# Batch 5's q by TensorE, batch 1's convolution on VectorE, four one-batch tap buffers and a new order in a fused attention and gated-convolution kernel

## The chip, the core and the metric

The kernel runs on one core of a Trainium2 chip. A core has TensorE (PE in the profile; it multiplies matrices into PSUM, and its loading of the stationary operand is listed as PEld), VectorE (DVE), ScalarE (ACT), GpSimd (POOL), SyncE (SP, here a queue for DMAs alone) and 16 DMA engines that move data between HBM and SBUF. Each engine works through its own queue of instructions in order, and engines wait for one another by semaphores. The metric is the device time of one execution in microseconds, the median of several runs.

## What is computed

The inputs are q, k, v of shape (8 batches, 8 heads, 576 tokens, 64), a norm weight g, and three weights of a gated convolution layer, all float32; the output is (8, 576, 512) float32.

```python
kv  = einsum('bhsd,bhse->bhde', k, v)              # linear attention, no softmax
out = einsum('bhsd,bhde->bhse', q, kv)
rms = sqrt(mean(out * out, axis=-1) + 1e-6)        # over the 64 of a head
x   = (out / rms * g) -> (batch, 576, 512)         # heads side by side
h   = maximum(x @ w_in, 0)                         # 512 -> 1024
conv = sum_k conv_w[k] * h shifted by k - 1 tokens # 3 taps, each channel by itself
y   = (h * sigmoid(conv)) @ w_out                  # 1024 -> 512
```

## The kernel before

All products are bf16 with float32 sums. The eight batches go through the same steps, and four pairs of batches share one x and one h buffer. Two heads fill the 128 rows of a tile, so a batch has four tiles t of x; h has eight tiles f of 128 channels.

The program is a list of small functions (`@op`, lines 216 to 795) and one string, `ORDER` (line 67). A token such as `kv.3.0.4@2` calls `kv(3, 0, 4)` with buffer or PSUM bank number 2; `:1` chooses the other engine for a step that ScalarE and VectorE can both do. Each engine issues its part of the tokens exactly in this order (lines 807 to 815 chain the instructions of an engine), so the string decides all that lies behind what. The number of a slot decides which earlier use of a buffer must have ended first.

The tokens, in the order of a batch's way:

- `Lq`, `Lk`, `Lv`, `Li`, `Lo`: loads of q, k, v (two buffers each) and of w_in and w_out, issued on POOL's queue, which also converts to bf16. Batch 0 is loaded in pieces by `pre`, batch 1 in halves.
- `unread`: products of a constant tile whose result nobody reads; `unread.3` is three of them (line 427).
- `kv` (line 358): sums of k times v over tokens; `kvc`, `kvn`, `ky` copy them from PSUM, `kx` moves halves by DMA.
- q must be turned so that its 64 is on the partitions. `qt0` and `qt` do it on TensorE (line 380), one token of six at a time; `qtp` does it two tokens at a time (line 388) for batches in `QP`; `dq` does it by a DMA transpose on SP's queue (line 436) for batches in `QD`. `qc0` and `qc` copy the turned q from PSUM.
- `ot` and, for batches in `QUAD` (both ways that give pairs of tokens), `oq` (line 464): q times kv. `sq` squares on ScalarE, `oc` copies the product to a float32 buffer (ring `o32`).
- The norm: batches 0 and 1 by `on`, `nl`, `mu0`. The others by `ss` (sums of squares, line 575), `ln` (reciprocal root on ScalarE), `sl` (VectorE splits the factors), `sp` (TensorE spreads them over partitions, line 603) and `mu` (VectorE multiplies, line 629). `dq`'s batch 7 gets its factors by DMAs (`fw`, `fr`).
- `hm` (line 640): eight products of w_in for one tile f; `re` is the relu (ScalarE, or VectorE with `:1`).
- The convolution works on a pair of tiles f: `ta` makes the two outer taps of one tile (VectorE), `aa` and `ab` add them and h, `sg` is the sigmoid (ScalarE), `mg` multiplies h by it (VectorE). `CONV` has five groups: batch 0, batch 1 and the pairs 2-3, 4-5, 6-7. Tiles 6 and 7 of batches 0 and 1 go another way: `cm` (line 731) makes the sum of taps on TensorE with diagonal matrices (`dg`), and `sg` reads it from PSUM.
- `om` (line 761): eight products of w_out for 128 rows of output, in two halves of four for the first and the last pair; `ea` copies the sum (ring `row`), `st` stores it on SP's queue. `oh`, `eh`, `sh` do the last rows in two column halves.

ScalarE loads a table when it goes from `nl` or `ln` to `sg` or back (line 213). The taps lie in two buffers for two batches each:

```python
taps = [consts.tile([P, 2, 2, 2, TW], BF16, name=f"taps{i}") for i in range(2)]
...
T["tap", c, f // 2] = taps[slots.pop(0)]
```

Of the kernel before, what the change touches and what calls it, by code (L numbers as in the profile page):

```python
# [59 lines left out]
QD = (5, 6, 7)  # L60
QP = (4,)
# [6 lines left out]
pre@0,0,0 unread.10@0 qt0.0.0@0 ps pn pi ca.k.0 ca.v.0 kv.0.0.1@1 kvc.0.0.1.0:1@0 ct@2 qt0.0.1@3 qc0.0.0:1@0  # L68
kvc.0.0.1.1 ot.0.0@0 qc0.0.1:1 unread.3@4 kv.0.1.1@3 Lq.1.0@1 pg sq.0.0@0 on.0.0@4 al.x0@0 al.h1@0 nl.0.0@0 pc
dg.7:1 kvc.0.1.1.0:1 dg.6:1 unread.1@6 qt0.0.2@2 kvc.0.1.1.1:1 ot.0.1@6 unread.3@3 kv.0.2.1@3 sq.0.1@1 mu0.0.0  # L70
al.x1@1 Li.1 al.h0@1 kvc.0.2.1.0:1 Li.3 qc0.0.2:1@1 kvc.0.2.1.1:1 on.0.1@4 nl.0.1@1 qt0.0.3@2 Lv.1.0@1 ot.0.2@0
mu0.0.1 sq.0.2@2 qc0.0.3:1 unread.3@3 kv.0.3.1@4,5 kvc.0.3.1.0 on.0.2@6 kvc.0.3.1.1:1 nl.0.2@2 ot.0.3@4 mu0.0.2
sqh.0.3.0@3 unread.3@3 onh.0.3.0@6 sqh.0.3.1 onh.0.3.1 nlh.0.3.0@3 muh.0.3.0 Lk.1.0@1 qt.1.0@0 nlh.0.3.1 qc.1.0:1@2
muh.0.3.1 Li.0 hm.0.2@6 re.0.2 ta.0.2@0 hm.0.3@4 re.0.3 hm.0.6@6 Lq.1.2 ta.0.3 Lv.1.2 re.0.6 aa.0.1 hm.0.7@4 Lk.1.2
Lq.2.0@0 cm.0.6@6 re.0.7:1 sg.0.6@1 kv.1.0.2@0 cm.0.7@4 kvc.1.0.2.0:1@1 kvc.1.0.2.1 sg.0.7 ot.1.0@0 hm.0.1@6 ab.0.1
sq.1.0@4 re.0.1 qt.1.1@4 hm.0.0@2 on.1.0@6 mg.0.3 qc.1.1@3 ot.1.1@4 nl.1.0@4 re.0.0:1 sq.1.1@5 kv.1.2.2@2
kvc.1.2.2.0 ta.0.0@1 mu0.1.0 kvc.1.2.2.1 on.1.1@6 Li.2 ot.1.2@2 nl.1.1@5 ot.1.3@0 ta.0.1 sq.1.2@6 mu0.1.1 aa.0.0
unread.1@6 on.1.2@6 sq.1.3@7 ab.0.0 nl.1.2@6 mu0.1.2 on.1.3@4 nl.1.3@7 Lk.2.0@0 qt.2.0@6 sg.0.3 qt.2.1@4 mu0.1.3
ha.1.2@2 hb.1.2 qc.2.1@4 sg.0.2 qc.2.0@0 ha.1.3@0 hb.1.3 re.1.2 re.1.3 hm.1.7@4 Lv.2.0@0 hm.0.4@2 mg.0.1 Lq.3.0@1
hm.0.5@0 sg.0.1 Lk.3.0@1 Lv.3.0@1 re.1.7 sg.0.0 pl ta.1.2@0 re.0.4 ta.1.3 re.0.5 hm.1.4@4 kv.2.0.4@2 Lo.0 aa.1.1  # L80
ab.1.1 mg.0.0 sg.1.3 sg.1.2 kvc.2.0.4.0@0 hm.1.5@0 kvc.2.0.4.1 ta.0.4@1 ta.0.5 ot.2.0@2 mg.1.1 aa.0.2 hm.1.6@6
re.1.4 ot.2.2@4 re.1.5 sq.2.0@0 ta.1.4@0 ab.0.2 re.1.6 qt.3.1@0 oc.2.0:1@0 qt.3.0@6 qc.3.1@1 hm.1.1@2 ot.2.1@0
# [10 lines left out]
st.0.0 ab.2.2 ta.2.6@0 sg.2.5 re.3.1 re.3.2 ta.2.7 oq.4.3@6 oq.4.2@0 sg.2.4 re.2.3 kv.5.0.4@5 sq.4.2@2 Lv.7.0@0
Lk.7.0@0 om.0.6.4 om.0.5.0@2 aa.2.3 ab.2.3 Lk.6.0@1 Lv.6.0@1 kvn.5.0.4 sq.4.3@3 oc.4.2@0 mg.2.2 ky.5.0.4.0:1
ea.0.6@4 ss.4@3 dq.7.0@1 oc.4.3 ky.5.0.4.1:1 oq.5.0@0 oq.5.1@4 sq.5.0@4 ta.2.2@1 om.0.5.4 sq.5.1@5 oc.5.0:1@2
om.0.4.0@6 oc.5.1 ta.2.3 oq.5.3@0 oq.5.2@4 aa.2.1 om.0.8.0@7 ea.0.5@5 ab.2.1 sq.5.3@6 om.0.4.4 sq.5.2@7 ss.5 ln.2@0
om.0.8.4 hm.2.1@2 oc.5.2@3 ea.0.8@6 oc.5.3 re.2.1 sl.2@0 hm.2.0@4 sp.4.1@0,2 ea.0.4@7 om.0.7.0@7 re.2.0 mu.4.1.0
mu.4.1.1 sp.4.0@4,0 kv.7.0.4@6 mu.4.0.0 sg.2.2 mu.4.0.1 om.0.7.4 kvn.7.0.4:1 sg.2.3 ea.0.7@2 sp.5.0@4,2 hm.3.0@0
al.h2@1 re.3.0 kx.7.0.4.0 dq.7.1@4 mu.5.0.1 mu.5.0.0 hm.4.5@2 re.4.5 sp.5.1@6,4 hm.4.1@0 mg.2.1 mu.5.1.0 hm.4.2@2
mu.5.1.1 ta.2.0@1 sg.2.7 hm.4.0@6 hm.5.3@4 ta.2.1 re.4.1 sg.2.6 mg.2.3 kx.7.0.4.1 re.4.0 re.4.2 oq.7.0@0 re.5.3  # L100
kv.6.0.4@6 oq.7.1@4 sq.7.0@0 hm.5.2@2 oc.7.0@1 aa.2.0 Lq.6.0@1 hm.4.3@0 st.0.4 dq.6.0@2 sq.7.1@1 oc.7.1 re.5.2
hm.4.4@4 st.0.5 kvn.6.0.4:1 ab.2.0 ta.3.2@0 re.4.3 hm.5.6@0 st.0.1 ta.3.3 hm.5.4@2 hm.5.1@6 sg.2.1 sg.2.0 re.4.4
re.5.6 re.5.1 re.5.4 hm.5.0@4 oq.7.3@6 oq.7.2@0 aa.3.1 re.5.0 mg.2.0 om.1.6.0@2 om.1.3.0@3 ab.3.1 st.0.3 kx.6.0.4.0
st.0.6 ta.3.0@1 dq.6.1@3 sq.7.3@2 sq.7.2@3 ta.3.1 sg.3.3 sg.3.2 hm.5.5@4 oc.7.2@0 st.0.7 aa.3.0 ss.7@0 mg.3.1 ln.4@0
al.x3@1 ab.3.0 ta.3.4@0 ea.1.3@7 re.5.5 om.1.1.0@1 oc.7.3 ea.1.6@5 kx.6.0.4.1 om.1.0.0@0 fw.4 fr.7.0@0 ea.1.1@0
oq.6.0@2 oq.6.2@6 oq.6.3@4 om.1.8.0@1 ta.3.5 ea.1.0@1 sq.6.2@4 fr.7.1@1 oc.6.2@2 oq.6.1@6 aa.3.2 om.1.4.0@0 sq.6.0@5
sq.6.3@6 sq.6.1@7 oc.6.0@3 ss.6@2 ab.3.2 oc.6.1 ea.1.8@4 ln.3@0 ea.1.4@2 hm.4.6@6 om.1.5.0@2 oc.6.3 sl.3@0 st.1.0
# [738 lines left out]
```

## Time and profile before

| | |
|---|---|
| three runs | 179.43, 179.44, 180.92 us |
| span of the profiled execution | 177.6 us |
| TensorE, busy | 168.4 us |
| ScalarE, busy | 149.7 us |
| VectorE, busy | 139.5 us |
| granted TensorE clock, every slice | 9 (90% or more of full speed) |

The span is the time from the first to the last instruction that the profiler recorded; the times of runs are those of whole executions, so they lie somewhat above it. Matmuls are pipelined and the profile models their ends, so mean times of single products overlap, and the step from one to the next is shorter. The chain of waits follows the work that ended last back to its start and gives start and length of each piece. In rows of groups stand line, engine, operation, output<-input, shapes, count, then busy time, mean ns of one, and idle time before them with what ended it.

### The profile page before, as it was taken

What the parts mean: (1) busy time and instruction counts of PE and PEld (TensorE: products, weight loads), DVE (VectorE), ACT (ScalarE), POOL (GpSimd) and SP (SyncE); (2) the same over time, 40 slices, a digit from 0 to 9 for tenths busy, and PEclk for the clock granted to TensorE, in tenths of its full rate; (3) what the DMA queues carried; (4) which work ended last, traced back from release to release, by engine and by line L of the source; (5) the groups of instructions that cost most, each with busy time, mean ns of one, the idle gap of its engine ahead of it and who ended that gap; (6) DMA issues with size and microseconds to landing.
All of it is one profiled execution on the core that took longest, in us unless ns stands there. A gap on an engine that the chain in (4) does not pass through costs nothing.

```text
span 177.6 us, 4060 instructions
## 1 busy us (share of the span) xinstructions
PE 168.4 (95%) x1641; PEld 101.3 (57%) x1660; DVE 139.5 (79%) x235; ACT 149.7 (84%) x233; POOL 30.8 (17%) x54
## 2 busy tenths in 40 slices
PE   6989996999999999999999999999999999999992
PEld 2545753877545677753667764444677764444541
DVE  5665669999998898999799999939999999950000
ACT  2479899999999969999999999999989987764332
POOL 7995516402600013050000000000000000000000
PEclk9999999999999999999999999999999999999999
DMA  6999999999999999999999950197040003422696
GB/s 155 188 183 197 200 204 201 205 203 206 205 204 203 198 192 139 174 203 198 160 201 179 293 128 0 53 219 263 21 160 0 4 0 143 152 82 99 258 352 219
DMA packets 36219, 29.49 MB, mean 166 GB/s; under 512 B 8528, under 2 KB 31720, under 8 KB 36200
## 3 DMA queue, kind: packets, MB, share of 16 engines
q0 software_dynamic: 21760, 15.96, 59.5%
q1 hardware_dynamic: 14400, 13.26, 28.9%
q8 instruction: 13, 0.21, 0.4%
q14 instruction: 6, 0.05, 0.1%
q10 hardware_dynamic: 40, 0.01, 0.0%
HBM read 33.70 MB, written 9.58 MB: 244 GB/s over the span
## 4 chain that ended last, share of the span: by engine, by line
PE 70%; DMA 20%; POOL 4%; ACT 2%; issue 2%; POOLq 0%; ACTq 0%
PE bank L761 33%; PE bank L640 27%; DMA v_sb<-in_v_dram 10%; DMA k_sb<-in_k_dram 7%; DMA q_sb<-in_q_dram 4%; PE bank L358 3%; PE bank L464 2%; POOL q_sb L241 1%; PE bank L603 1%; PE bank L575 1%; POOL v_sb L241 1%; POOL k_sb L241 1%; PE bank L776 1%; PE bank L731 1%; PE bank L388 1%
## 5 line engine op out<-in xcount | busy, mean ns | idle before, releaser
L640 PE MATMUL bank<-xT,w_in_sb 128*128 128x288 bf16 x496 | 64.5, 286 | 0.1
L761 PE MATMUL bank<-w_out_sb,h 128*128 128x512 bf16 x268 | 63.0, 379 | 1.1 <-issue 0.6
L640 PEld LDWEIGHTS <-w_in_sb 128*128 128x128 bf16 x496 | 47.6, 98 | 14.1 <-issue 0.5
L761 PEld LDWEIGHTS <-h 128*128 128x128 bf16 x280 | 26.3, 98 | 30.6 <-issue 1.9
L646 ACT ACTIVATE h<-bank 128x576 bf16<-128x576 f32 x61 | 37.9, 657 | 4.2 <-PE bank L640 3.9
L745 ACT ACTIVATE taps<-taps,cwn 128x1152 bf16<-128x1152 bf16 (+1 forms) x36 | 38.2, 1094 | 0.1
L341 ACT ACTIVATE row<-bank 128x512 f32<-128x512 f32 (+1 forms) x37 | 21.3, 598 | 12.3 <-PE bank L761 9.3
L751 DVE TENSOR_TENSOR h<-h,taps 128x2304 bf16<-128x2304 bf16 (+1 forms) x20 | 22.2, 1113 | 2.0 <-ACT taps L745 1.2
L706 DVE TENSOR_TENSOR taps<-taps 128x2304 bf16<-128x2304 bf16 (+1 forms) x18 | 20.9, 1160 | 0.4
L712 DVE TENSOR_TENSOR taps<-taps,h 128x2304 bf16<-128x2304 bf16 (+1 forms) x18 | 20.8, 1153 | 0.3
L699 DVE TENSOR_SCALAR taps<-h,cwn 128x1152 bf16<-128x1152 bf16 (+1 forms) x36 | 16.7, 463 | 2.5 <-ACT h L646 2.4
L493 ACT ACTIVATE sq<-bank 128x576 bf16<-128x576 f32 x28 | 17.9, 676 | 0.0
L700 DVE TENSOR_SCALAR taps<-h,cwn 128x1152 bf16<-128x1152 bf16 (+1 forms) x36 | 17.5, 487 | 0.0
L629 DVE SCALAR_TENSOR_TENSOR xT<-o,cw,bank 128x576 bf16<-128x576 f32 x20 | 15.3, 809 | 2.7 <-PE bank L603 2.5
L341 ACT ACTIVATE o<-bank 128x576 f32<-128x576 f32 x22 | 15.0, 694 | 0.0
L213 ACT ACT_TABLE_LOAD x10 | 12.8, 1283 | 2.5 <-issue 2.4
L301 POOL DMA_DIRECT2D q_sb<-in_q_dram x8 | 6.2, 772 | 31.4 <-PE bank L388 16.6
L427 PE MATMUL bank<-fill 128*128 128x512 bf16 x25 | 9.0, 480 | 1.7 <-DVE fill L228 1.5
L358 PEld LDWEIGHTS <-k_sb 96*64 96x64 bf16 x384 | 7.3, 114 | 4.0 <-issue 2.6
L358 PE MATMUL bank<-v_sb,k_sb 96*64 96x64 bf16 x384 | 8.5, 199 | 1.0 <-DMA k_sb<-in_k_dram 0.7
L301 POOL DMA_DIRECT2D k_sb<-in_k_dram x8 | 6.1, 758 | 14.4 <-PE bank L358 12.5
L562 DVE SCALAR_TENSOR_TENSOR xT<-bank,cw,root 128x576 bf16<-128x576 f32 x7 | 5.6, 815 | 1.8 <-ACT root L542 1.7
(93 smaller groups left out, 135.3 us busy)
## 6 DMA issues: line engine op xcount, KB each, us to landing
out_dram<-row SPq DMA_DIRECT2D x35, 256.0 KB, 2.8
q_sb<-in_q_dram POOLq DMA_DIRECT2D x6, 576.0 KB, 13.7
k_sb<-in_k_dram POOLq DMA_DIRECT2D x6, 576.0 KB, 14.7
v_sb<-in_v_dram POOLq DMA_DIRECT2D x6, 576.0 KB, 16.3
factor<-factor SPq DMA_DIRECT2D x4, 288.0 KB, 4.9
w_in_sb<-in_moe_w_in_dram POOLq DMA_DIRECT2D x4, 256.0 KB, 8.7
w_out_sb<-in_moe_w_out_dram POOLq DMA_DIRECT2D x2, 512.0 KB, 18.0
q_sb<-in_q_dram POOLq DMA_DIRECT2D x4, 144.0 KB, 4.6
```

The costliest lines, as they stand in the source:

```text
L341: nc.scalar.activation(to, fr, AX.Copy)
L358: nc.tensor.matmul(ps[i][i * D:(i + 1) * D, t - t0, :], k_sb[:, 2 * t + i, r * D:(r + 1) * D], v_sb[:, 2 * t + i, r * D:(r + 1) * D], star ...
L493: nc.scalar.activation(in_order(b, s), product(b, t), AX.Square)
L640: nc.tensor.matmul(ps[:, e, :HS], w_in_sb[:, t, f * P:(f + 1) * P], x[:, t, e * HS:(e + 1) * HS], start=(t == 0), stop=(t == NT - 1))
L646: nc.scalar.activation(to, fr, AX.Relu)
L699: nc.vector.tensor_scalar_mul(tap[:, 0, f % 2, :n, 8:8 + S], h[:, f], cwn[:, 0, f:f + 1])
L700: nc.vector.tensor_scalar_mul(tap[:, 1, f % 2, :n, :S], h[:, f], cwn[:, 2, f:f + 1])
L706: nc.vector.tensor_add(tap[:, 1, :, :n, :S], tap[:, 0, :, :n, 7:7 + S], tap[:, 1, :, :n, 1:1 + S])
L712: nc.vector.tensor_add(y, y, h[:, 2 * j:2 * j + 2])
L745: nc.scalar.activation(y, y, AX.Sigmoid, scale=cwn[:, 1, f:f + 1])
L751: nc.vector.tensor_mul(h, h, T["tap", c, j][:, 1, :, :n, :S])
L761: nc.tensor.matmul(T["om", p, m], h[:, f, m * P:(m + 1) * P], w_out_sb[:, f, :], start=(f == 0), stop=(f == NF - 1))
```

## The change

Batch 5 goes from `QD` to `QP`: its q is turned on TensorE two tokens at a time, and copied by two `qc`, instead of two DMA transposes. The sum of taps of batch 1's tiles 6 and 7 is made on VectorE by `ta`, `aa`, `ab` like the others, instead of `cm` on TensorE. The tap buffers become four for one batch each; a group of two batches takes two that are neighbours. Output rows 0 to 511 of the last pair go to the float32 buffers of `oc`. The whole order is written anew: among other things fifteen groups of unread products (39 in all) stand where eight groups (27) stood, and ScalarE's table changes twelve times, not ten.

```diff
-QD = (5, 6, 7)
-QP = (4,)
+QD = (6, 7)
+QP = (4, 5)
...
 ORDER = """
-pre@0,0,0 unread.10@0 qt0.0.0@0 ps pn pi ca.k.0 ca.v.0 kv.0.0.1@1 kvc.0.0.1.0:1@0 ct@2 qt0.0.1@3 qc0.0.0:1@0
...
-oc.2.1 Lk.4.0@0 Lv.4.0@0 kv.3.0.4@2 re.1.0 ss.2@3 oc.2.3 mg.0.2 ln.8@0 aa.1.2 kvc.3.0.4.0:1@1 kvc.3.0.4.1:1 ab.1.2
...
-om.0.2.0@2 Lv.5.0@1 sg.1.5 sg.1.4 qtp.4.0@0 cm.1.6@6 qc.4.0@4 mg.1.2 ea.0.0@2 hm.2.5@4 sl.1@0 hm.2.2@0 sg.1.1
-om.0.2.4 re.2.5 sg.1.6@0 re.2.2 ea.0.2@3 sg.1.0 sp.3.0@6,4 cm.1.7@0 mu.3.0.1 mu.3.0.0 hm.2.4@2 hm.2.7@6 sg.1.7
...
-st.3.2 st.3.0 st.3.7 eh.3.8.1 sh.3.8.1
+pre@0,0,0 unread.10.0@0 ca.v.0 Lq.1.0@1 unread.3.5@1 pi ca.k.0 qt0.0.0@0 unread.1.3@1 kv.0.0.1@2 qc0.0.0@0
...
+sq.2.1@3 qc.3.0@0 ss.2@4 kv.3.0.4@5 qc.3.1@1 ln.8@0 hm.1.1@6 kvc.3.0.4.0@0 ab.1.1 kvc.3.0.4.1 oc.2.0:1@1 Lo.1 sl.8@0
...
+om.0.2.0@6 om.0.2.4 qtp.4.0@2 sg.1.0 ta.1.5 mu.2.0.0 Lv.4.0@0 mu.2.0.1 ea.0.2@3 sl.1@0 qtp.5.1@0 ab.1.3 qtp.5.0@4
...
+kvn.4.0.4 hm.2.6@2 mu.3.1.1 ky.4.0.4.0:1 re.2.6 Lq.7.0@1 qtp.4.1@0 ky.4.0.4.1:1 hm.3.4@4 sg.1.6 qc.4.1@3 sg.1.5 re.3.4
...
+sg.4.5 ta.4.7 om.3.2.0@2 st.2.4 st.1.1 ea.2.8@3 om.2.2.0@6 sg.4.4 aa.4.3 st.2.5 om.3.7.0@3 ab.4.3 ea.2.0@2 om.3.5.0@4
+ea.2.2@4 sg.4.7 om.3.4.0@5 sg.4.6 om.3.3.0@6 mg.4.2 ea.2.1@6 om.3.1.0@7 st.1.0 st.2.2 om.3.0.0@1 ea.2.3:1@0 mg.4.3
+om.3.0.4 st.2.6 om.3.5.4 om.3.3.4 om.3.7.4 ea.3.5:1@4 ea.3.0@0 oh.3.8.0@0 om.3.1.4 st.2.7 ea.3.7:1@1 ea.3.3@1 om.3.4.4
...
+oh.3.8.1 ea.3.4:1@3 st.3.1 st.3.4 st.3.2 ea.3.6@4 eh.3.8.1:1 st.2.3 st.3.6 sh.3.8.1
 """
...
+    def units(n):
+        s = slots.pop(0)
+        return taps[:, s:s + n].rearrange("p b k f w -> p k f b w")
...
-    taps = [consts.tile([P, 2, 2, 2, TW], BF16, name=f"taps{i}") for i in range(2)]
+    taps = consts.tile([P, 4, 2, 2, TW], BF16, name="taps")
...
-        for t in taps:
-            nc.vector.memset(t[:, 0, :, :, 7:8], 0.0)
-            nc.vector.memset(t[:, 1, :, :, S:S + 1], 0.0)
+        nc.vector.memset(taps[:, :, 0, :, 7:8], 0.0)
+        nc.vector.memset(taps[:, :, 1, :, S:S + 1], 0.0)
...
-    def unread(n):
+    def unread(n, i=0):
...
-            T["tap", c, f // 2] = taps[slots.pop(0)]
+            T["tap", c, f // 2] = units(CONV[c][1])
...
-        T["os", p, m] = ring("row", [P, S], FP32, name="row")[:, :D_model]
+        T["os", p, m] = ring("o32" if p == 3 and m < 4 else "row", [P, S], FP32, name="row")[:, :D_model]
```

By the new order the steps that move from ScalarE to VectorE are eight relus, four `oc`, seven `ea` and one `eh`; two `kvn` and three `kvc` move the other way. Three of four `qc0`, all on ScalarE before, are on VectorE now; of the `qc`, one of eight was on ScalarE and three of ten are. Batch 7's q is loaded into buffer 1, which batch 5 had, instead of buffer 0; `Li.2` is ahead of `Lq.2`, and `Lv.3` ahead of `Lq.3` and `Lk.3`.

More of the change, by code (lines that the diff above doesn't have):

```diff
@@ L67 @@
 ORDER = """
-pre@0,0,0 unread.10@0 qt0.0.0@0 ps pn pi ca.k.0 ca.v.0 kv.0.0.1@1 kvc.0.0.1.0:1@0 ct@2 qt0.0.1@3 qc0.0.0:1@0
[L69 to L82, printed above, removed]
@@ L93 @@
[L93 to L107, printed above, removed]
@@ L739, in sg @@
             if f % 2 == 0:
-                T["tap", c, f // 2] = taps[slots.pop(0)]
+                T["tap", c, f // 2] = units(CONV[c][1])
             y = T["tap", c, f // 2][:, 1, f % 2, 0, :S].rearrange("p (e n) -> p e n", e=2)
```

64 lines of the change are left out of this document (45 added, 19 removed).

## The prediction

> **What bounds the kernel now.** I read the page first, then the three stretches into which two waits for loads cut the span, then the chain of waits and the timeline of TensorE. The page:
>
> ```profile
> PE 168.4 (95%) x1641; PEld 101.3 (57%) x1660; DVE 139.5 (79%) x235; ACT 149.7 (84%) x233; POOL 30.8 (17%) x54
> DMA  6999999999999999999999950197040003422696
> PE 70%; DMA 20%; POOL 4%; ACT 2%; issue 2%; POOLq 0%; ACTq 0%
> ```
>
> TensorE is busy for 95% of the span, but a fifth of the chain that ended last is loads, and the DMA row is full for the first 22 slices. The timeline of TensorE says where loads decide:
>
> ```profile
> 1.47 4.45 PE L427 MATMUL bank<-fill 128*128 128x512 bf16 x10 [1.47 <-DVE fill L228]
> 10.58 0.81 PE L427 MATMUL bank<-fill 128*128 128x512 bf16 x3
> 27.04 0.57 PE L358 MATMUL bank<-v_sb,k_sb 96*64 96x64 bf16 x24 [0.72 <-DMA k_sb<-in_k_dram]
> 45.91 0.95 PE L358 MATMUL bank<-v_sb,k_sb 96*64 96x64 bf16 x48 [0.19 <-DMA v_sb<-in_v_dram]
> ```
>
> The k-v products of batch 1's second half (27.04) and of batch 3 (45.91) waited for their loads. Cut there, the view of stretches (time, PE, PEld, DVE, ACT, POOL busy, clock, DMA) reads:
>
> ```profile
> 0.00:27.04 27.04, 24.00 (x273) 13.78 (x276) 17.34 (x57) 18.85 (x30) 17.25 (x29) 1.00 1.20 188
> 27.04:45.91 18.87, 17.26 (x264) 12.57 (x268) 18.39 (x35) 18.50 (x33) 7.18 (x17) 1.00 1.32 204
> 45.91:174.26 128.35, 127.17 (x1106) 74.98 (x1119) 103.72 (x145) 112.00 (x171) 6.38 (x8) 1.00 0.77 156
> ```
>
> Behind 45.91 TensorE is idle for 128.35 - 127.17 = 1.18 us only, until its last product at 174.26; 3.3 us of the 177.6 us span follow (last copy and store). So the time is: the landing of batch 3's loads, plus TensorE's work behind it, plus 3.3. I set the profiled execution beside the median of 179.44, so 1.8 us lie around its span, and I carry differences over unchanged.
>
> **The first 46 us.** The new order has the same loads ahead of batch 3's products (q, k, v of four batches, w_in); only their sequence differs, so by bytes batch 3 lands at the same time. Li.2 goes ahead of Lq.2, and all of Lv.3, Lq.3, Lk.3 still wait for products of batch 1 alone. POOL's queue gets the nine memsets of sel ahead of Lk.2, while earlier loads are still under way. TensorE gets 12 more unread products ahead of 27.04 (35 for 23). Three follow the first ten: 4.45/10 = 0.445 each, 1.3 us; nine at 0.81/3 = 0.27 are 2.4 us; 3.7 in all. The stretch has 27.04 - 24.00 = 3.04 us of idle, 1.47 of them ahead of the first product, so 1.57 can swallow some and TensorE is at worst 2.1 us late at 27.04. From there to 45.91 it had 1.61 us idle; its work there changes by one w_in product group less (0.98, row below), ss.2 (0.36) and three unread more (0.8): +0.2. At worst batch 3's products start 0.7 us late. I take 0: these products mostly stand where TensorE waits for landing loads anyway, and if that cover goes they cost 0.7.
>
> **TensorE behind 45.91.** The chain of waits has a row for every step that changes:
>
> ```profile
> 46.86 0.36 PE bank L575 x8
> 47.22 0.32 PE bank L427
> ...
> 47.59 0.38 PE bank L427
> ...
> 51.94 1.73 PE bank L761 x8
> ...
> 56.54 0.51 PE bank L388 x12
> 57.05 0.74 PE bank L731 x6
> ...
> 60.85 0.85 PE bank L731 x6
> ...
> 64.82 0.62 PE bank L388 x12
> ...
> 88.23 0.88 PE bank L358 x48
> ...
> 108.90 0.98 PE bank L640 x8
> ...
> 166.46 0.87 PE bank L776 x8
> ```
>
> - Batch 1's convolution leaves TensorE: cm.1.6 and cm.1.7, 0.74 + 0.85 = -1.59.
> - Batch 5's q comes by 24 transposes of two tokens, like batch 4's 24 in the rows: 0.51 + 0.62 = +1.13.
> - hm.1.1 slips behind batch 3's products, +0.98; ss.2 moves ahead of them, -0.36; the last unread group goes, -0.70.
>
> Sum -0.54: work 126.63. With the old idle of 1.18, TensorE ends at 45.91 + 126.63 + 1.18 = 173.72 instead of 174.26. The clock has nothing to give there: it is granted at 1.00 in the whole stretch.
>
> **VectorE behind 45.91.** Here the price is hidden. In the rows (busy, mean ns):
>
> ```profile
> L706 DVE TENSOR_TENSOR taps<-taps 128x1152 bf16<-128x1152 bf16 x6 | 4.5, 757 | 0.1
> L700 DVE TENSOR_SCALAR taps<-h,cwn 128x576 bf16<-128x576 bf16 x12 | 4.8, 398 | 0.0
> L343 DVE COPY qT<-bank 128x1152 bf16<-128x1152 bf16 x7 | 5.1, 752 | 0.6 <-PE bank L380 0.5
> L648 DVE TENSOR_SCALAR h<-bank 128x576 bf16<-128x576 f32 x3 | 2.3, 753 | 0.3 <-PE bank L640 0.3
> L343 DVE COPY o<-bank 128x576 f32<-128x576 f32 x2 | 1.5, 754 | 0.2 <-ACT sq L493 0.2
> L343 DVE CAST kvbd<-bank 64x256 bf16<-64x256 f32 x2 | 0.8, 422 | 0.2 <-PE bank L358 0.2
> ```
>
> Until mg.4.3, the product that the last w_out sums wait for, VectorE gets behind 45.91: seven relus (0.753 each, 5.27), four oc (0.754, 3.02), three copies of output rows (no such row on VectorE; between 0.422 and 0.754, and 512 of 576 columns of the latter give 0.67: 2.0), two ab, one aa and one mg of one batch (0.755, 3.02), one ta (two instructions, not over 0.398 each: 0.80), one qc (0.75), less four copies of k-v sums (0.42, -1.69). Sum +13.17: 103.72 + 13.17 = 116.9 us. TensorE meets the first half sum that reads mg.4.3 with nine half sums (4 x 0.216 each) and two split ones (0.87) still to do, 9.5 us ahead of its end, at 173.72 - 9.5 = 164.2. So VectorE has 118.3 us for 116.9: it may idle for 1.4 us. Before, its last instruction ended at 158.89, and it idled for 112.98 - 103.72 = 9.26 us of that:
>
> ```profile
> 45.91:158.89 112.98, 111.91 (x1030) 67.47 (x1042) 103.72 (x145) 106.26 (x161) 6.38 (x8) 1.00 0.78 143
> 86.72:128.20 41.48, 41.16 (x389) 24.23 (x393) 37.96 (x53) 41.39 (x62) 0.00 (x0) 1.00 0.72 150
> 120.00:140.00 20.00, 19.95 (x150) 13.82 (x150) 19.89 (x28) 18.67 (x27) 0.00 (x0) 1.00 0.27 96
> 157.53 1.36 DVE L751 TENSOR_TENSOR h<-h,taps 128x2304 bf16<-128x2304 bf16 x1 [1.20 <-ACT taps L745]
> ```
>
> How much it will idle is the unknown. Low end: the densest stretch, 0.11 of 20 us, gives 0.65 us in 118. High end: 86.72 to 128.20, with the factors of two batch groups in it, 3.52 of 41.48, gives 10. I take 2.5, nearer the dense row, because with more work queued, fewer of its waits find it empty; a factor (sl, mu) that waits for ScalarE or TensorE still holds up everything behind it on VectorE's queue. The excess over 1.4 is 1.1 us, which TensorE must wait. The four one-batch buffers let four one-batch taps stand at once; I count nothing for them beyond this.
>
> ```profile
> L213 ACT ACT_TABLE_LOAD x10 | 12.8, 1283 | 2.5 <-issue 2.4
> ```
>
> Behind 45.91 ScalarE loses eighteen relus and copies and gains eight smaller instructions and two table loads (2 x 1.283 = 2.6). Of 128.35 us it was busy for 112.0, so it stays below TensorE.
>
> The output rows of the last pair move to the o32 buffers; stores that held up ScalarE there held up no TensorE step, so 0. The last copy goes to VectorE: 0.422 for ScalarE's like copy, nothing. Forecast: 179.44 - 0.54 + 1.1 = 180.0.
>
> **Loads behind 45.91.** Batch 5's two DMA transposes go. Lq.7 now takes batch 5's buffer and waits for batch 5's transposes, which stand in the order where 12 us of TensorE work have followed 45.91, so it issues near 58 instead of 65.74, with five loads queued behind it. On SP's queue dq.7.0 is now first and holds st.0.0 and st.0.1 until q of batch 7 has landed; their buffers are wanted much later. What transposes cost the loads is in the timelines of POOL and SP and the times to landing (the three answers are in the order of POOL's three issues):
>
> ```profile
> 27.91 0.77 POOL L301 DMA_DIRECT2D k_sb<-in_k_dram  x1 [2.10 <-PE bank L358]
> 43.47 0.77 POOL L301 DMA_DIRECT2D q_sb<-in_q_dram  x1 [10.25 <-PE bank L380]
> 65.74 0.77 POOL L301 DMA_DIRECT2D q_sb<-in_q_dram  x1 [16.55 <-PE bank L388]
> 56.40 7.41 SPq L436 DMA_TRANSPOSE qT<-q_sb  x2
> 63.86 0.58 SPq L795 DMA_DIRECT2D out_dram<-row  x1
> k_sb<-in_k_dram POOLq DMA_DIRECT2D x1, 576.0 KB, 14.5
> q_sb<-in_q_dram POOLq DMA_DIRECT2D x1, 576.0 KB, 12.8
> q_sb<-in_q_dram POOLq DMA_DIRECT2D x1, 576.0 KB, 12.4
> ```
>
> From 42.4 to 56.3 five loads landed, 2.8 each; from 56.3 to 78.1, with two transposes and one store among them, five more at 4.4: 7.8 us for these three, about 3.5 a transpose. In the new kernel k of batch 7 is the ninth load behind 56.3: 56.3 + 9 x 2.8 = 81.5, plus one transpose of batch 7 (3.5) and three stores (0.8 each, what I leave them of the 7.8): 87.4. TensorE wants it at about 87.5, 0.7 us earlier than its 88.2 before. It may just wait, at most for a second transpose, 3.5 us; I take 0. [...]
>
> **Rivals.**
> 1. VectorE becomes the bound (slower). For it: three engines now need about the same time, and 86.72 to 128.20 shows 8.5% idle. Against it: 120 to 140 shows 0.5%. It decides the sign of the verdict once VectorE idles more than 3.8 us (3.2%) between 45.91 and mg.4.3. Midway between the ends, 5.3 us, the excess is 3.9: 179.44 - 0.54 + 3.9 = 182.8; the high end gives 187.5.
> 2. Batch 7's loads come late: 1.5 us on the forecast, 181.5; against it, the estimate above that just meets.
> 3. Everything fits and loads come earlier: the idle of 1.18 goes and batch 3 lands a little sooner (0.2): 179.44 - 0.54 - 1.18 - 0.2 = 177.5. Against it: those 1.18 us are many short gaps between groups of products, which nothing in the change touches.
>
> **How the numbers follow.** The forecast (TensorE bound, VectorE up to 3.8 us idle, 178.9 to 181.2) has 0.49, rival 1 0.33, rival 2 0.08, rival 3 0.10. A measurement of this kernel tells about 1% (1.8 us) from no change. Faster is rival 3 alone: 0.10. Slower is rival 1 and a good third of rival 2 (0.03): 0.36. The rest is 0.54. The range cuts off rival 3 and the upper third of rival 1: 177.8 to 183.6.
>
> **What would show it.** Batch 3's products start at 45.9 with a short wait for a load; if they start later and wait for none, the early unread products cost time. TensorE's busy time behind them is 126.6. VectorE's is near 117 until mg.4.3, and the waits of w_in and w_out products for VectorE sum to about 1 us; 4 us or more make rival 1 right. A wait of batch 7's products for k_sb makes rival 2 right. If TensorE idles for under 0.5 us behind 45.9, my view of VectorE is wrong. The whole is wrong if the first 46 us change by more than 1 us either way.

## The result, and the profile after

The changed kernel takes 183.31 us in the median of 20 runs (180.97 to 189.78), the kernel before 179.89 us in 20 runs beside them (178.98 to 181.92); the ratio is 1.0082, with a 95% interval of 1.006 to 1.0104. That ratio is smaller than that of the two medians because half of the changed kernel's runs lie near 181 us and half from 184 us up, and the comparison, here and in the experiments, leaves out runs that lie more than 1.5% above the fastest of their kernel.

The page of the first profile, which is one of the upper half (span 186.0 us, execution 187.78 us): busy times of the engines, the granted clock, the DMA engines' busy share in 40 slices, and the shares of the chain that ended last.

```profile
PE 174.0 (94%) x1684; PEld 103.5 (56%) x1684; DVE 153.5 (83%) x257; ACT 144.8 (78%) x219; POOL 30.6 (16%) x54
PEclk9999999999999999999958999999999999999998
DMA  6999999999999999999943640039460000236494
PE 72%; DMA 19%; DVE 5%; POOL 1%; issue 1%; DVEq 0%
```

VectorE did get the work: 139.5 us before, 153.5 now. But VectorE has 5% of the chain, and the loads have 19% of it. The clock row, which was full before, has a 5 just past the middle. The timeline of TensorE (start, length, what was done, and in brackets the idle time before it and who ended it) shows where:

```profile
47.53 0.95 PE L361 MATMUL bank<-v_sb,k_sb 96*64 96x64 bf16 x48 [0.44 <-DMA k_sb<-in_k_dram]
93.35 1.49 PE L361 MATMUL bank<-v_sb,k_sb 96*64 96x64 bf16 x48 [4.64 <-DMA k_sb<-in_k_dram]
```

Batch 3's k-v products start at 47.53 (45.91 before). Batch 7's start at 93.35 (88.23 before), after 4.64 us in which TensorE waits for batch 7's k. The stretches of the same profile (time, then busy time of PE, PEld, DVE, ACT, POOL, granted clock, DMA share, GB/s): up to that wait, behind it, all of it, and the half-clock part by itself.

```profile
47.53:88.71 41.18, 41.17 (x472) 24.94 (x472) 40.19 (x67) 40.69 (x70) 7.42 (x10) 1.00 1.32 191
93.35:182.19 88.84, 88.76 (x656) 51.67 (x656) 74.90 (x97) 66.59 (x92) 0.00 (x0) 0.97 0.37 118
47.53:182.19 134.66, 129.94 (x1128) 76.61 (x1128) 116.32 (x165) 109.64 (x163) 7.42 (x10) 0.97 0.69 143
92.39:99.21 6.82, 5.86 (x68) 3.22 (x68) 1.54 (x2) 2.35 (x4) 0.00 (x0) 0.50 0.64 146
```

Apart from the one wait TensorE idles for 0.01 us of the first stretch and 0.08 us of the second. So behind batch 3's products no wait for VectorE is left to look for. A second profile of the same kernel caught a run of the lower half (span 179.4 us, execution 181.23 us); its timeline, and then its stretch behind batch 3's products:

```profile
46.90 0.95 PE L361 MATMUL bank<-v_sb,k_sb 96*64 96x64 bf16 x48
89.37 0.95 PE L361 MATMUL bank<-v_sb,k_sb 96*64 96x64 bf16 x48 [1.14 <-DMA k_sb<-in_k_dram]
```

```profile
46.90:175.60 128.70, 127.49 (x1132) 75.53 (x1128) 116.72 (x166) 109.74 (x163) 7.90 (x11) 1.00 0.69 149
```

Here the wait is 1.14 us, and the clock stays at 1.00. This profile closes the account against the kernel before (span 177.6): batch 3's products 0.99 us later; TensorE behind them, without the wait, 128.70 - 1.14 = 127.56 instead of 128.35, so -0.79; the wait +1.14; behind the last product 179.4 - 175.6 = 3.8 instead of 3.34, so +0.46. The sum is +1.80, and 179.4 - 177.6 = 1.8.

The first profile adds to the same items a wait of 4.64 and the stretch at half clock: from batch 7's products to the last one it takes 88.84 us, where the second takes 175.60 - 89.37 = 86.23, so 2.61 us more for 6.82 us at a clock of 0.50.

### The profile page after: what moved, and what is told of

The parts are those of the page before. It is cut to its first block, busy times and chain, and to the rows that moved or that the text cites. A ratio compares the mean times of both kernels' runs of the same rounds, so it can differ in the third digit from the quotient of the medians.

```text
span 186.0 us, 4141 instructions
## 1 busy us (share of the span) xinstructions
PE 174.0 (94%) x1684; PEld 103.5 (56%) x1684; DVE 153.5 (83%) x257; ACT 144.8 (78%) x219; POOL 30.6 (16%) x54
## 4 chain that ended last, share of the span: by engine, by line
PE 72%; DMA 19%; DVE 5%; POOL 1%; issue 1%; DVEq 0%
PE bank L764 29%; PE bank L643 24%; DMA k_sb<-in_k_dram 19%; PE bank L430 6%; PE bank L361 4%; PE bank L434 2%; PE bank L383 1%; PE bank L606 1%; DVE h L651 1%; PE bank L391 1%; PE bank L467 1%; PE bank L779 1%; POOL v_sb L304 1%; PE bank L734 1%; DVE taps L709 1%
## 5 line engine op out<-in xcount | busy, mean ns | idle before, releaser
L643 PE MATMUL bank<-xT,w_in_sb 128*128 128x288 bf16 x496 | 66.3, 289 | 0.1
L764 PE MATMUL bank<-w_out_sb,h 128*128 128x512 bf16 x280 | 65.0, 383 | 0.0
L748 ACT ACTIVATE taps<-taps,cwn 128x1152 bf16<-128x1152 bf16 (+1 forms) x38 | 40.3, 1079 | 5.6 <-DVE taps L715 5.6
L649 ACT ACTIVATE h<-bank 128x576 bf16<-128x576 f32 x53 | 34.0, 658 | 5.5 <-PE bank L643 5.2
L344 ACT ACTIVATE row<-bank 128x512 f32<-128x512 f32 (+1 forms) x29 | 16.3, 590 | 10.5 <-PE bank L764 9.4
L632 DVE SCALAR_TENSOR_TENSOR xT<-o,cw,bank 128x576 bf16<-128x576 f32 x20 | 15.4, 809 | 8.6 <-ACT kvn L344 5.4
L703 DVE TENSOR_SCALAR taps<-h,cwn 128x1152 bf16<-128x1152 bf16 (+1 forms) x38 | 17.8, 468 | 0.0
L702 DVE TENSOR_SCALAR taps<-h,cwn 128x1152 bf16<-128x1152 bf16 (+1 forms) x38 | 17.5, 462 | 0.2 <-ACT h L649 0.2
L217 ACT ACT_TABLE_LOAD x12 | 15.4, 1283 | 2.6 <-issue 2.4
L430 PE MATMUL bank<-fill 128*128 128x512 bf16 x39 | 13.3, 463 | 1.5 <-DVE fill L232 1.5
L344 ACT ACTIVATE o<-bank 128x576 f32<-128x576 f32 x18 | 11.9, 670 | 0.0
L346 DVE COPY row<-bank 128x512 f32<-128x512 f32 (+1 forms) x8 | 5.3, 656 | 7.4 <-PE bank L764 4.5
L651 DVE TENSOR_SCALAR h<-bank 128x576 bf16<-128x576 f32 x11 | 8.3, 752 | 1.1 <-PE bank L643 1.0
```

What stands on the lines that cost most here:

```text
L344: nc.scalar.activation(to, fr, AX.Copy)
L430: nc.tensor.matmul(ps[:, :512], fill[:, :P], fill, start=True, stop=True)
L643: nc.tensor.matmul(ps[:, e, :HS], w_in_sb[:, t, f * P:(f + 1) * P], x[:, t, e * HS:(e + 1) * HS], start=(t == 0), stop=(t == NT - 1))
L649: nc.scalar.activation(to, fr, AX.Relu)
L703: nc.vector.tensor_scalar_mul(tap[:, 1, f % 2, :n, :S], h[:, f], cwn[:, 2, f:f + 1])
L748: nc.scalar.activation(y, y, AX.Sigmoid, scale=cwn[:, 1, f:f + 1])
```

## The experiments

All ratios are against runs of the kernel before on the same chip, with 95% intervals. The first four experiments ran on one chip, the next four on a second and the last four on a third, so between these groups ratios compare better than medians. Where nothing else is said, an edit is made to the changed kernel.

### The changed kernel again

> The changed kernel as it is, profiled once more. In its first profile batch 3's k-v products started at 47.53 us (45.91 in the kernel before), batch 7's at 93.35 (88.23 before) after 4.64 us in which TensorE waited for the load of k; behind the wait the granted clock was 0.50 for 6.83 us; TensorE's busy time behind 47.53 was 129.94 of 134.66 us. Theory A (the time is lost to loads: batch 3's about 1.6 us late, batch 7's between 0 and 4.6 us late): here again batch 3 starts at 47.0 to 47.6, TensorE has under 0.5 us of idle behind it apart from the wait ahead of batch 7's products, and the span moves from profile to profile with that wait alone. Theory B (VectorE and ScalarE are the bound, as the prediction's first rival has it): TensorE idles for over 2 us in waits for VectorE or ScalarE behind batch 3's products.

183.48 us, ratio 1.0119 (1.0072 to 1.0166). This is the second profile above: batch 3's products at 46.90, a wait of 1.14 for k, under 0.1 us of other idle. Theory A holds; of theory B's waits of over 2 us there is nothing. The start of batch 3's products moved by 0.6 us between two profiles of one kernel, without a load being waited for in the second, so it varies by itself.

### One transpose of batch 7's q later

```diff
-sq.5.2@7 ss.4@3 oc.5.2@3 ss.5 om.0.8.4 dq.7.1@0 ln.2@0
+sq.5.2@7 ss.4@3 oc.5.2@3 ss.5 om.0.8.4 ln.2@0
...
-kx.7.0.4.0 mu.5.0.0
+kx.7.0.4.0 dq.7.1@0 mu.5.0.0
```

> The changed kernel with the second DMA transpose of batch 7's q issued behind batch 7's k-v products instead of about 17 us ahead of them. Theory A (two transposes and three stores take DMA time from the loads of v of batch 6 and k of batch 7, at about 3.5 us a transpose by the prediction's estimate): k of batch 7 lands about 3 us earlier than in the changed kernel, the wait ahead of batch 7's products is under 1.5 us, and the median falls by 1 to 3 us, to within 0.3% of the time of the kernel before plus 1.0 us. Theory B (VectorE and ScalarE are the bound): no change (within 0.3%), the time only moves from one wait to another.

179.83 us, ratio 0.9983 (0.9953 to 1.0013): the 0.8 to 1.2% are gone, and of 12 runs one lies above 181.2. One token is worth that much. The issues of POOL and SP in the first profile of the changed kernel show what it had stood in the way of:

```profile
73.99 0.77 POOL L304 DMA_DIRECT2D v_sb<-in_v_dram  x1 [6.57 <-PE bank L467]
74.81 0.77 POOL L304 DMA_DIRECT2D k_sb<-in_k_dram  x1
...
72.28 1.84 SPq L439 DMA_TRANSPOSE qT<-q_sb  x1
74.17 1.58 SPq L798 DMA_DIRECT2D out_dram<-row  x3
75.94 6.41 SPq L439 DMA_TRANSPOSE qT<-q_sb  x1
```

A transpose, three stores and the second transpose are issued on SP's queue within 4 us of the last two loads that TensorE is waiting for. The profile of this experiment still has a wait of 1.10 us, with k landing at 88.80 instead of 89.33: its execution, 180.64 us, is the third slowest of the twelve, so the size of the gain is read from the runs and not from that profile. The load of k took 14.96 us from issue to landing there, and 15.01 in the second profile of the changed kernel, so no trace shows that this load is faster without the transpose.

### Twelve unread products fewer, and both edits together

The tokens unread.3.5@1, unread.1.3@1, unread.2.5@7, unread.3.2@6, unread.1.1@6, unread.1.2@7 and unread.1.4@4 go, which leaves 23 products ahead of batch 1's second k-v products.

> The changed kernel with 23 unread products ahead of batch 1's second k-v products instead of 35, as many as the kernel before has; nothing else is moved. Theory A1 (the twelve products make TensorE late at 27.04, so that the buffers of batch 1 come free late and batch 3's loads are issued late): batch 1's second k-v products start near 27.0 instead of 28.1, batch 3's loads are issued 1 us earlier and land by 46.4, batch 3's products start 1.1 us earlier, and the time falls by 0.5 to 1.1 us (0.3 to 0.6%). Theory A2 (batch 3's loads are late because the DMA moves fewer bytes between 31 and 47 us, whatever TensorE does): batch 3's products start within 0.3 us of 47.5 and the time stays within 0.2%. Fewer products early may also lower the granted clock: then it is below 1.00 in the first 10 us.

186.17 us, ratio 1.0313 (1.0274 to 1.0351). Less work, and 3% slower. The timeline of TensorE, and then two stretches of 2 us (DMA share and GB/s are the last two numbers) and the one at half clock:

```profile
45.70 0.95 PE L361 MATMUL bank<-v_sb,k_sb 96*64 96x64 bf16 x48
91.56 1.36 PE L361 MATMUL bank<-v_sb,k_sb 96*64 96x64 bf16 x48 [4.53 <-DMA k_sb<-in_k_dram]
```

```profile
70.00:72.00 2.00, 2.00 (x64) 1.49 (x61) 2.00 (x3) 2.00 (x5) 0.00 (x0) 1.00 1.31 203
78.00:80.00 2.00, 2.00 (x11) 0.78 (x8) 1.87 (x4) 2.00 (x5) 0.00 (x0) 1.00 1.61 87
91.79:95.20 3.41, 3.41 (x56) 1.90 (x51) 1.54 (x2) 0.44 (x2) 0.00 (x0) 0.50 0.68 107
```

Batch 3's products start 1.20 us earlier than in the second profile, as theory A1 said, but TensorE then comes to batch 7's products earlier as well, and k is not there: it was issued 1.2 us earlier (73.12 instead of 74.31) and landed 2.2 us later (91.52 instead of 89.33). While loads and a transpose run together, from 78 to 80 us, the DMA engines move 87 GB/s, against 203 from 70 to 72. Behind the wait of 4.53 us the clock falls to 0.50 in this profile, and the mean granted clock of each of the six runs, 0.977 to 0.991, fits a fall in all of them. Neither theory had that.

Both edits:

> Both edits together. Theory A with A1: the gains add, 1.5 to 4 us off the changed kernel, to between 0.5% faster and 0.5% slower than the kernel before. Theory A with A2: the same as with the late transpose alone. Theory B: no change from the changed kernel.

182.83 us, ratio 1.0033 (0.9991 to 1.0076). The gains do not add: six of the twelve runs lie above 183. Even with the later transpose the profile, of one of these six (span 182.3), has a wait of 3.50 us for k, which took 17.36 us to land, and a clock of 0.50 from 91.57 to 95.00.

### Batch 7's k loaded ahead of batch 6's v

Both loads wait for the same products of batch 5, so they can change places at no cost.

```diff
-hm.2.1@0 Lv.6.0@1 ea.0.8@5
+hm.2.1@0 Lk.7.0@1 ea.0.8@5
...
-sp.4.1@0,6 Lk.7.0@1 om.0.7.0@4
+sp.4.1@0,6 Lv.6.0@1 om.0.7.0@4
```

> The changed kernel with the load of batch 7's k issued ahead of the load of batch 6's v; both wait for the same buffers, so only their sequence changes. In the second profile of the changed kernel v of batch 6 landed at 83.99 and k of batch 7 at 89.33 us, wanted at 88.23; v of batch 6 is wanted about 4.4 us later. Theory A (the wait for this k, and the half clock behind a long wait, are what the time varies with): k lands 3 to 5 us earlier than v did not, by about 86, the wait ahead of batch 7's products goes, batch 6's products wait under 1 us, no run is above 182.5, the median falls to 179.8 to 180.6. What is left over the kernel before is batch 3's products, 1.0 us late. Theory B (DMA transposes and loads together are too slow in sum, the sequence does not matter): batch 6's products wait as long as batch 7's did, and the time stays.

179.74 us, ratio 0.9979 (0.995 to 1.0009); one of 12 runs is above 180.7, where theory A said that none would be above 182.5 (it is 183.24). Two answers on single DMA issues (to landing, in us, in the last column) say why: first the load of k in the second profile of the changed kernel, then in this one. After them, of this kernel, TensorE's batch 7 products in the timeline and the stretch behind batch 3's products:

```profile
k_sb<-in_k_dram POOLq DMA_DIRECT2D x1, 576.0 KB, 15.0
```

```profile
k_sb<-in_k_dram POOLq DMA_DIRECT2D x1, 576.0 KB, 12.0
```

```profile
87.81 0.95 PE L361 MATMUL bank<-v_sb,k_sb 96*64 96x64 bf16 x48
```

```profile
46.54:174.05 127.51, 126.60 (x1120) 75.53 (x1128) 116.71 (x166) 109.54 (x163) 7.93 (x11) 1.00 0.72 152
```

Issued at 73.16, k is there at 85.1; TensorE waits for no load at 87.81. The v of batch 6 landed at 89.88, before it was wanted at 92.19. Nothing of the transposes, the stores or VectorE's work was touched, and the loss is gone: the sequence of two loads was enough, and theory B falls. (This stretch has 8 fewer matmul records than the weight loads say, so its 126.60 is a little low; its length is not affected.)

### Fewer unread products, now that k is in time

> The same with 23 unread products ahead of batch 1's second k-v products instead of 35. With the fewer products alone batch 3's products started at 45.70 us instead of 46.90, and the wait for k of batch 7 grew to 4.53 us. Theory A: the 1.2 us now stay gained where k lands in time. It is wanted at 87.0 and v of batch 6 had landed at 87.7 in that kernel, so a wait of 0 to 1 us is left: median 178.6 to 179.8, faster than the kernel before or equal. Theory C (the unread products keep the clock up, and fewer of them cost time by the clock itself): the granted clock falls below 1.00 in the first 30 us and the time is above that of the kernel with all of them.

180.27 us, ratio 0.9994 (0.9962 to 1.0027): no gain over k first alone, and not the 178.6 to 179.8 of theory A. The profile, of the fastest of the twelve runs, has batch 3's products at 45.90 and no wait for k, but k lands at 85.74 and is wanted at 87.2, a margin of 1.4 us that is smaller than what its landing varies by in these profiles; the twelve runs go from 179.01 to 182.68. Theory C finds nothing: the clock is 1.00 in this profile's first 30 us.

### All that has helped, together

To k first and the fewer unread products come the later transpose, the stores st.0.0 and st.0.1 behind kx.7.0.4.0, and the last copy on ScalarE again (eh.3.8.1 without its :1).

> The same as the last, and also: the second transpose of batch 7's q and the stores of output rows 0 to 255 of the first pair behind the move of batch 7's sums, and the last copy on ScalarE instead of VectorE. Theory A: k of batch 7 lands by 85, TensorE has no wait ahead of batch 7's products, batch 3's start at 45.7, TensorE's 127.6 us follow and 3.4 to 3.8 us behind them: span 176.7 to 177.3, median 178.5 to 179.1 (0.5 to 0.8% under the kernel before). Rival V (VectorE is next: in the changed kernel its last factor, mg.4.3, ended at 165.57 and TensorE wanted it at about 166.1, 0.5 us later): with TensorE ahead by 2 us, it waits for mg.4.3 for up to 1.7 us, a span near 178.3 and a median near 180.

178.42 us, ratio 0.9913 (0.9881 to 0.9946): faster than both kernels, all eleven runs between 177.98 and 180.10. Behind batch 3's products:

```profile
46.08:173.60 127.52, 126.61 (x1120) 75.51 (x1128) 116.70 (x166) 109.51 (x163) 7.91 (x11) 1.00 0.71 152
```

The span is 176.9, which is 46.08 + 127.52 + 3.3. The stretch is as long as with k first alone, so rival V has no wait here; against the profile of k first the gain is the start, 0.46 us earlier, and the end, 3.3 us behind the last product instead of 3.8. The load is in time by more than 4 us (k lands at 83.16, and its products start at 87.35), which fits the narrow spread of the runs.

### Three relus more for VectorE

On top of k first, re.6.0, re.6.3 and re.7.2 get a :1.

> The kernel with k of batch 7 loaded first, and three relus of the third pair (tiles 0 and 3) and of the fourth (tile 2) on VectorE instead of ScalarE: 3 x 0.75 = 2.26 us more for VectorE, behind batch 7's products and ahead of mg.4.3. By the prediction's view (VectorE idles for 2.5 us at least and has no slack) TensorE waits 2.3 us longer: 1.3% above the kernel with k first. By the traces (mg.4.3 ended 0.5 us ahead of its use, and VectorE idled for some 4.7 us between batch 3's products and its end): the idle swallows part of it, TensorE waits 0 to 1.7 us. By the view that VectorE is no bound at all: no change within 0.2%.

186.67 us, ratio 1.0342 (1.0302 to 1.0381): 6.9 us more than k first, three times the added work, and more than any of the three views gave. The timeline, first TensorE, then VectorE, and the stretch at half clock:

```profile
137.34 2.08 PE L643 MATMUL bank<-xT,w_in_sb 128*128 128x288 bf16 x8 [4.74 <-DVE h L651]
...
132.28 0.75 DVE L651 TENSOR_SCALAR h<-bank 128x576 bf16<-128x576 f32 x1
132.94 0.81 DVE L628 SCALAR_TENSOR_TENSOR xT<-o,cw,factor 128x576 bf16<-128x576 f32 x1
133.67 0.52 DVE L702 TENSOR_SCALAR taps<-h,cwn 128x1152 bf16<-128x1152 bf16 x1
134.10 0.52 DVE L703 TENSOR_SCALAR taps<-h,cwn 128x1152 bf16<-128x1152 bf16 x1
134.53 0.81 DVE L628 SCALAR_TENSOR_TENSOR xT<-o,cw,factor 128x576 bf16<-128x576 f32 x1
135.26 1.36 DVE L709 TENSOR_TENSOR taps<-taps 128x2304 bf16<-128x2304 bf16 x1
136.53 0.75 DVE L651 TENSOR_SCALAR h<-bank 128x576 bf16<-128x576 f32 x1
```

```profile
134.67:141.50 6.83, 4.16 (x18) 2.58 (x18) 5.82 (x6) 0.78 (x2) 0.00 (x0) 0.50 0.00 0
```

Between the relu at 132.28 and the one at 136.53, which frees the bank that TensorE waits for, VectorE has five instructions of the norm and the taps in its queue. The wait ends with it, at 137.34, and again 6.83 us at half clock lie around its end; the 4.16 us of them behind the wait cost half, so 4.74 + 2.08 make 6.8 of the 6.9. So a VectorE that holds TensorE up does show itself in a wait for VectorE; the changed kernel has none. And the sum of work was not what decided: the place in the queue was.

### Batch 1's convolution on TensorE again

On top of k first: ta.1.6, ta.1.7, aa.1.3 and ab.1.3 go, cm.1.6@2 comes ahead of hm.2.7, cm.1.7@6 behind hm.3.4, and sg.1.6 and sg.1.7 follow them.

> The kernel with k of batch 7 first (median 179.74 us), and in it the sum of taps of batch 1's tiles 6 and 7 on TensorE again, as in the kernel before. TensorE gets 0.74 + 0.85 = 1.59 us, VectorE loses two pairs of outer taps (1.6) and one aa and one ab (0.76 each), 3.1 us. TensorE as the bound (it idled for under 0.2 us behind batch 3's products): 1.0 to 1.6 us slower, 0.6 to 0.9%. VectorE as the bound: up to 1 us faster.

181.99 us, ratio 1.0135 (1.0115 to 1.0156): 2.25 us more than k first by the medians and 2.8 by the ratios, above the 1.0 to 1.6 expected. In the profile (batch 3's products at 46.02) the stretch behind them is 130.01 instead of 127.51, with two short waits in the timeline:

```profile
46.02:176.03 130.01, 128.89 (x1144) 76.87 (x1140) 115.80 (x164) 109.34 (x163) 7.91 (x11) 1.00 0.69 150
```

```profile
61.56 0.90 PE L734 MATMUL bank<-h,dgw 128*128 128x288 bf16 x6 [0.51 <-ACT h L649]
70.80 3.10 PE L643 MATMUL bank<-xT,w_in_sb 128*128 128x288 bf16 x24 [0.59 <-ACT h L649]
```

Of the 2.50, 1.10 are two waits for ScalarE, which come from where the two steps had to be put in this order; 1.40 are left for the products themselves (1.59 expected). TensorE is the bound, VectorE isn't, and this part of the change was worth its price.

### Batch 5's q by DMA transposes again

On top of k first, QD and QP as before; dq.5.1@1 and dq.5.0@2 stand where qtp.5.1 and qtp.5.0 stood, both qc.5 go, and q of batch 7 and of batch 6 change buffers.

> The kernel with k of batch 7 first, and in it batch 5's q by two DMA transposes again, as in the kernel before; q of batch 7 goes to batch 4's buffer as it did there. TensorE loses 24 transposes, 1.13 us. By the prediction's 3.5 us that a transpose takes from the loads, k of batch 7 lands 7 us later than at 85.1, at 92, and TensorE, which wants it at about 86.7, waits 5 us and has a stretch at half clock behind that: 4 to 6 us slower. [...]

182.28 us, ratio 1.012 (1.0077 to 1.0163): 2.5 us more than k first, less than the 4 to 6 expected. The timeline of TensorE:

```profile
88.87 0.95 PE L361 MATMUL bank<-v_sb,k_sb 96*64 96x64 bf16 x48 [1.07 <-DMA k_sb<-in_k_dram]
95.32 0.95 PE L361 MATMUL bank<-v_sb,k_sb 96*64 96x64 bf16 x48 [0.99 <-DMA v_sb<-in_v_dram]
```

k landed at 88.83, 3.7 us later than with k first, not 7. What the expectation forgot: with the loads late, the three stores, which stand on SP's queue behind the first transpose of batch 7's q, are late too. They are issued from 78.56 on and the first of them lands at 89.91, so none is ahead of this k any more. The last load in the queue, q of batch 6, lands at 98.92 instead of 92.98, with the same three stores ahead of it. So the two transposes cost up to 5.9 us together, about 3.0 each, an estimate; in the profiles with both transposes of batch 7 and all three stores that load landed anywhere from 91.64 to 95.37, which makes it 1.8 to 3.6. TensorE waits 1.07 us for k and not 5, and no stretch at half clock follows (1.00 from 85 to 100 us), but it also waits 0.99 us for v of batch 6, which is late as well.

### The twelve unread products in the fastest kernel

> The fastest kernel so far (178.42 us: k of batch 7 first, second transpose and two stores later, last copy on ScalarE, 23 early unread products) with the 35 early unread products of the change. If the twelve products cost TensorE what the first pair of profiles showed, 1.2 us: 179.6. If they only fill waits for loads, as the prediction had it, batch 3's products start 0 to 0.4 us later and the median is 178.4 to 178.9. If they keep the clock up, it is below 178.4.

179.19 us, ratio 0.9985 (0.9956 to 1.0014), where without them it was 0.9913. Batch 3's products start at 46.74, 0.66 us later than with 23. This profile, of the third slowest of the twelve runs, also has a wait of 1.0 us for a transposed q. So here the twelve cost, by 0.7% (1.3 us) with intervals that nearly touch; with k in time but tight they cost nothing (the pair above).

### Two stores later

st.0.0 and st.0.1 go behind kx.7.0.4.0, nothing else is changed.

> The changed kernel with the stores of output rows 0 to 255 of the first pair issued behind the move of batch 7's sums instead of 17 us ahead of its products; loads and transposes as in the change. By the prediction's terms (0.8 us of loads a store) k of batch 7 lands 1.6 us earlier than in the changed kernel: the wait of 1.1 to 4.6 us shrinks to 0 to 3 us, and the runs above 184 become few; median 180.3 to 182. If the transposes alone hold the loads up, the time stays at 183.5 (0.3%).

182.62 us, ratio 1.0028 (0.9994 to 1.0062), with runs from 179.17 to 185.21; two of 11 are above 184, as against 10 of the 20 and 4 of the 12 of the changed kernel. Better, but not mended, and the median is above the 180.3 to 182 expected: in the profile k lands at 90.48, later than the 89.33 of the second profile and not 1.6 us earlier, and TensorE waits 2.00 us. The second transpose, which stood behind the stores on SP's queue, is now issued at 73.25 instead of 75.11: with two of the stores gone from ahead of it, it started 1.86 us earlier. The 0.8 us a store of the prediction is not shown by this run or another.

## Why the prediction was right or wrong

The forecast was 180.0, 0.3% slower, by a VectorE that makes TensorE wait; the kernel came out 0.8% slower in the comparison and 183.31 in the median, by a load that came late. The sign held and the reason did not. That the time lies in the range is luck: the 1.1 us of waiting for VectorE did not come, and the wait for k, 1.14 us in the second profile, which the forecast had at 0, happens to be of the same size.

**The first 46 us: the bound was taken to be the loads, and it was not.** The prediction took 0 for the early unread products, at worst 0.7 us, since they stand where TensorE waits for loads. Batch 3's products start at 45.99 to 47.18 in eight profiles of kernels with 35 of them (46.54 in the mean), and at 45.70 to 46.08 in the four with 23 (45.93). So the cost is about 0.6 us, the worst end of the step. (The first profile's 47.53 is not counted; it did wait for its load.) The chain of waits shows the reason (start, length, engine and line). Before, two loads led up to batch 3's products:

```profile
15.16 11.83 DMA k_sb<-in_k_dram
...
28.67 17.11 DMA v_sb<-in_v_dram
```

In the second profile of the changed kernel no load is in the chain ahead of them. It goes from the unread products to VectorE, and at the end from squares on ScalarE to the sums ss.2, which now stand ahead of batch 3's products:

```profile
1.47 5.59 PE bank L430 x13
...
30.55 0.72 DVE xT L565
...
32.61 0.74 DVE xT L565
33.39 0.65 PE bank L658 x4
...
45.32 1.09 ACT sq L496 x2
46.54 0.43 PE bank L578 x8
46.97 0.88 PE bank L361 x48
```

The stretch of it in which VectorE decides:

```profile
28.00:34.00 6.00, 5.24 (x66) 3.16 (x61) 6.00 (x12) 5.46 (x10) 3.86 (x5) 1.00 1.32 204
```

VectorE is busy for 6.00 of 6.00 us there. The load of k, by its landing at 45.24, would have let batch 3 start 1.7 us earlier than 46.90. The prediction looked for a busy VectorE only behind 45.91; it came ahead of it. Its own test (later, and waiting for no load) said so.

**TensorE behind 45.91: held.** Predicted -0.54 of work with the old idle of 1.18 kept, measured -0.79 to -0.84 for work and idle together (127.56 and 127.51 against 128.35). So the sum was right to 0.3 us. Its split into work and idle was not, and the old idle of 1.18 was for the most part never idle. Behind 45.91 the kernel before has 1106 records of products for 1119 weight loads, and its gaps of 0.16 us stand where a record is missing, as in this half sum, of whose four products three are listed:

```profile
55.73 0.81 PE L761 MATMUL bank<-w_out_sb,h 128*128 128x512 bf16 x3 [0.16 <-issue]
```

With k first 8 records are missing and 0.91 us look idle; in the second profile none is missing and 0.07 us are idle beside the wait, at the same length. So rival 3, by which these 1.18 us would go, had next to nothing to gain there. The convolution's share, 1.59, measured 1.40 by itself.

**VectorE: the step that failed.** Predicted: 116.9 us of work until mg.4.3, 2.5 us of idle, so TensorE waits 1.1 us. The profile with k first has VectorE's stretch up to its last factor, and two of its neighbouring instructions:

```profile
46.54:164.10 117.56, 116.70 (x1068) 70.45 (x1076) 113.94 (x162) 106.77 (x158) 7.93 (x11) 1.00 0.72 143
162.64 1.36 DVE L754 TENSOR_TENSOR h<-h,taps 128x2304 bf16<-128x2304 bf16 x1 [0.69 <-ACT taps L748]
```

The work is 113.94 us, 3.0 less than the sum of 21 added and four removed instructions gave; the factor ends at 164.00, and 164.00 - 46.54 - 113.94 = 3.52 us are idle, 1.0 more than was taken. TensorE ends at 174.05, so by the prediction's 9.5 us it wants the factor at 164.55. The slack is 0.55 us, where the prediction had a lack of 1.1. Part of the 3.0 is that means were added as if instructions stood end to end. The second profile shows how far they overlap:

```profile
148.86 1.36 DVE L715 TENSOR_TENSOR taps<-taps,h 128x2304 bf16<-128x2304 bf16 x1
150.13 1.35 DVE L754 TENSOR_TENSOR h<-h,taps 128x2304 bf16<-128x2304 bf16 x1
```

The step from one to the next is 1.27, the length 1.36: 0.09 less for each instruction, 1.5 for a net 17. The rest is mostly overlap too: counted from each start to the next, the net 17 instructions add 11.8 us, and those that both kernels have take 1.6 us less than before. Rival 1 did not happen, by 0.55 us. The wait that the three relus made, at 137.34, is 27 us ahead of this factor and comes from a place in the queue, so what lies beyond this edge was not measured.

**Loads: rival 2, which had a chance of 0.08, is what happened.** The prediction had k of batch 7 land at 87.4, with one transpose and three stores ahead of it, and put a second transpose at up to 3.5 us but took 0 for it. It landed at 89.33 and 93.31 in the two profiles. In the second profile the nine loads start behind 56.2 (q of batch 5 lands), as predicted. The first five of them land 2.9 us apart, which makes 26.1 for nine and leaves 7.0 us for transposes and stores, and 9.2 in the first profile (from 58.01). The prediction had 5.9 there, with one transpose; with two it would have had 9.4. So this term was too small, and by the times of the runs it was the 0 for the second transpose: dq.7.1 is issued at 75.94 and 75.11, right behind the last loads, and taking it away from there gave back all of the loss. The traces do not show that link: with k still behind v, it took 14.96 and 17.36 us to land in the two profiles without that transpose, and 15.01 with it in the second profile. Only with two stores gone as well, in the fastest kernel, is the last load early, at 88.47 instead of 92.98 with k first. What the traces do show is that the order decides: ahead of v of batch 6, with both transposes and all three stores left, k lands at 85.12. The price of a transpose, 3.5, is inside the 1.8 to 3.6 that the experiment with batch 5's q gives. Also, the prediction noted that k comes as the ninth load but not that it could have been ahead of v of batch 6, which is wanted 4.4 us later.

**The clock: not in the prediction.** It stated that the clock had nothing to give, and did not ask what a longer wait would take. Waits of up to 2.00 us left it at 1.00 in every profile; waits of 3.50, 4.53, 4.64 and 4.74 us each brought a stretch at 0.50. That is what one profile shows of the upper half of the changed kernel's runs, and their clocks agree: the mean granted clock of a run is 0.968 to 0.991 in the ten upper ones and 0.995 to 1.0 in the others.

**The end: mis-sized, and the cause is open.** The last copy on VectorE was put at nothing. The span behind the last product went from 3.34 to 3.8 in the second profile, and to 3.3 in the fastest kernel, where the copy is on ScalarE again. But it is about 3.3 as well in the profiles of batch 5's q by DMA transposes and of two stores later, which have the copy on VectorE. So the 0.46 us are measured, and that the copy makes them is not shown.

**What stays open.** Why the same load takes 10.5 to 15.4 us from issue to landing (v of batch 6 in the second profile and in the kernel with fewer unread products), when the bytes around it are the same, was not settled, and with it what the second transpose does to k: the traces show a lower rate (in the kernel before 102 GB/s where it had been 192) in part of the time in which loads and a transpose run together, not what sets when it falls. No profile shows a run near 179 us of the kernel with the later transpose.

## What to carry to other kernels

List the last transfers ahead of each step of the bottleneck engine with the time at which each is wanted, and put the one that is wanted first first; a swap of two loads took 1% off the time here. Price a wait by its length: here waits of up to 2.00 us cost themselves, and those of 3.50 us and more up to 2.6 us on top, because the clock fell. Where three engines are near the bound, ask for an added instruction what stands ahead of it in its queue, not only whether the engine has time in sum.

## What the runs showed of the hardware

A TensorE that idled for 3.50 us (both edits together) got half its clock 0.84 us after it had started again, at 91.57; one that idled for 4.74 us (three relus more) got it 2.07 us into the wait. The half-clock stretches lasted 3.43, 3.41, 6.82 and 6.83 us for the waits of 3.50, 4.53, 4.64 and 4.74. What sets the moment of the drop and the length of a stretch is not shown.

DMA transposes from SBUF to SBUF landed 3.6 us after their issue with no load under way (issued at 103.13 in the first profile of the changed kernel), 8.8 us with loads under way (issued at 72.28 in the same profile), and 10.7 and 16.0 us with loads under way in the kernel before (issued at 56.40 and 58.31). With packets of loads and of a transpose under way the DMA engines moved 192 GB/s from 64 to 66 us and 102 from 68 to 70, in the kernel before; with loads alone, from 56 to 58, they moved 205.
